# Where V's high and low parts lie in SBUF: interleaved, eight bytes between columns, in tiles half of 256 bytes further on

## The chip, the cores and the metric

The kernel runs on one core of a Trainium2 chip. The metric is device time in microseconds, the median of several executions. One execution is profiled; its rows are what the sections below quote.

## The reference

Eight batches of 3136 tokens go through an attention without softmax and then through a routed feed-forward part. Cut to what matters here:

```python
scores = (1 / S) * z @ z.T              # z: 3136 x 64
attn = np.maximum(scores, 0.0) ** 2     # 3136 x 3136
x = u * (attn @ v)                      # v: 3136 x 256
# then, per batch: the 128 tokens with the largest x @ w_gate go through
# relu(xe @ w1) @ w2, are weighted by a sigmoid, and are added back
```

By far the most work is in `attn @ v`: for each batch a product of 3136 x 3136 with 3136 x 256.

## The kernel before

Numbers are float32. To keep their precision in TensorE's faster float32 form, each operand is split into a high part and a low part (`split`: a copy that rounds gives the high part, a subtraction gives what is left). A product is then made of high times high, high times low and low times high, three matmuls that add into one PSUM bank.

Per batch, the tokens are cut twice. The columns of the score matrix are cut into seven chunks, five of 512 tokens, one of 256 and one of 320; a chunk is the moving operand's width of a matmul. The rows are cut into 24 pairs of 128-token tiles and a last half tile. One chunk with one pair of tiles is a slot, so there are 25 slots in a chunk. In each slot `scores` (line 440) makes the scores of a later slot, with slices of `ZH` and `ZL` as weights and a chunk of `Z` as the moving operand. ScalarE takes the relu and the square out of PSUM and rounds it (`hi`, lines 450 and 451), VectorE or GpSimd subtracts (`lo`, line 518). Since the score matrix is symmetric, about half of the squares are not computed again but stored to DRAM, transposed, and fetched back (`qk`, cast at line 418).

`mix` (line 556) then does the slot's twelve matmuls of `attn @ v`. V is the weight operand, 128 tokens by 128 features at a time; the squares `hi` and `lo` are the moving operand. For each of the two tiles and each half of the features there are three matmuls: V's high part with `hi`, V's low part with `hi`, V's high part with `lo`. Each matmul has a weight load of its own.

`prep_v` (lines 293 to 310) fills V. A tile of the pool `vpool` holds two token tiles: first the high parts of all 512 columns (2 x 256 features), then the low parts of the same columns, 2048 bytes each. ScalarE writes the high part, GpSimd the low part (for the first few tiles VectorE does). `V[b, j][:, w, h]` is what `mix` loads: part `w` (0 high, 1 low), feature half `h`, 128 columns that lie next to each other, 512 bytes.

Tiles are laid out pool after pool in the order in which the code makes them. Six constants (`c_sb`, `k_sb`, `w_bc`, `w_run`, `c16`, `w_col`) stand first in the pool `const`, then the expert's weights `wh` and `wl`, then `ZH`, `ZL` and `Z`, then `vpool`, and behind it the pools with `hi` and `lo`. Laid out so, `wh`, `wl`, `ZH`, `ZL`, `Z`, all twelve V tiles, `hi` and `lo` start at a multiple of 256 bytes within a partition.

The order of the instructions on each engine is written out by the program: a table of slots, with loads and preparations placed so many slots ahead, and all DMAs of the attention on SyncE's queue.

Of the kernel before, what the change touches and what calls it, by code (L numbers as in the profile page):

```python
# [10 lines left out]
F32 = mybir.dt.float32  # L11
F32R = mybir.dt.float32r
BF16 = mybir.dt.bfloat16
I32 = mybir.dt.int32
# [4 lines left out]
P = 128  # L19
CH = 512  # L20
GT = 4
Q = 32
# [66 lines left out]
def attention_then_routed_ffn(ctx: ExitStack, tc: tile.TileContext, zt, ut, v, wg, w1, w2, cst, cst16, keys, outs, at, cap):  # L89
# [8 lines left out]
    NK = D // P  # L98
# [10 lines left out]

    const = ctx.enter_context(tc.tile_pool(name="const", bufs=1))  # L110
    vpool = ctx.enter_context(tc.tile_pool(name="vpool", bufs=NJ // 2))
    stage = ctx.enter_context(tc.tile_pool(name="stage", bufs=2))
    work = ctx.enter_context(tc.tile_pool(name="work", bufs=2))
    tail = ctx.enter_context(tc.tile_pool(name="tail", bufs=2))
# [8 lines left out]
    def split(src, hi, lo, hi_on=None, lo_on=None):  # L123

        (hi_on or nc.scalar.copy)(hi, src)  # L125
        (lo_on or nc.vector.tensor_tensor)(lo, src, hi.bitcast(F32), op=ALU.subtract)  # L126
# [3 lines left out]
    staged = {}  # L130

    small = {
        "c_sb": const.tile([P, cst.shape[1]], F32, name="c_sb"),
        "k_sb": const.tile([P, keys.shape[1]], I32, name="k_sb"),
        "w_bc": const.tile([P, D], F32, name="w_bc"),
        "w_run": const.tile([P, RUN], F32, name="w_run"),
        "c16": const.tile([P, cst16.shape[1]], BF16, name="c16"),
        "w_col": const.tile([P, NK], F32, name="w_col"),
    }

    def load_consts():
# [59 lines left out]
    for o in range(0, W, 2 * D):  # L201
        kk, f = divmod(o, F)
# [16 lines left out]
    V = {}  # L219
# [74 lines left out]
    def prep_v(b, g, on=None):  # L294

        st = staged["v", b, g // 2][:, g % 2 * 2 :]
        n = 2 if 2 * g < NJ else 1
        if n == 2:
            t = vpool.tile([P, 2, NK, 2 * P], F32R, name="V", tag="V")
        else:  # L300
            t = vpool.tile([P, 2, NK, P], F32R, name="Vr", tag="Vr", bufs=1)
        src = st[:, :n].rearrange("p a d -> p (a d)").rearrange("p (f h i) -> p h f i", h=NK, i=Q)
        parts_of = [t[:, w].rearrange("p h (f i) -> p h f i", i=Q) for w in range(2)]
        lo_on, took = on or nc.gpsimd, {"dve": 1.0} if on else {"act": 0.6, "pool": 1.3}
        if not on and b == 0 and n == 2 and busy["pool"] + 1.3 > busy["dve"] + 0.6:
            lo_on, took = nc.vector, {"act": 0.6, "dve": 0.6}
        split(src, *parts_of, on and on.tensor_copy, lo_on.tensor_tensor)
        for q in range(n):
            V[b, 2 * g + q] = t[:, :, :, q * P : (q + 1) * P]
        spend(**took)  # L310


# [56 lines left out]
    def spend(act=0.0, dve=0.0, pool=0.0):  # L369
        busy["act"] += act  # L370
        busy["dve"] += dve
        busy["pool"] += pool
# [929 lines left out]
    for b in range(B):  # L1302
# [18 lines left out]
        for g in range(NJ // 2 + 1):  # L1321
            k = k0 - 10 + 3 * g // 2 if b else max(1, g - 3)
            if b or g > 3:
                at_slot(k, lambda b=b, g=g: prep_v(b, g))
            if (b or g > 6) and g % 2 == 0:
                load = (k - (3 if b else 2), lambda b=b, g=g: stage_v(b, g // 2))
                if b or 2 * g < NJ:
                    loads.append(load)
                else:
                    at_slot(*load)  # L1330
# [78 lines left out]
    def start():  # L1409
# [14 lines left out]
        prep_z(0, 1, hi_on=nc.vector.tensor_copy)  # L1424
        more_scores(0)
        prep_v(0, 0, nc.vector)
        busy["pool"] = 99.0
        settle_scores()
        more_scores(1)
        prep_v(0, 1)  # L1430
        square_scores()
        prep_z(0, 2, 1)
# [153 lines left out]
```

## Time and profile before

| | |
|---|---|
| median of 3 runs | 2068.55 us (2066.93 to 2069.06) |
| profiled execution, its time | 2067.41 us |
| its span, first to last instruction | 2065.6 us |
| TensorE busy, matmuls | 2055.2 us, 99% |
| TensorE busy, weight loads (beside the matmuls) | 1744.5 us, 84% |
| VectorE, ScalarE, GpSimd busy | 1529.0, 1291.2, 1357.5 us |

The busy time of matmuls is the time in which at least one is under way from its start to its modelled end, and a matmul starts while the one before it is still draining. So 99% says that there are almost no gaps; it does not say at what pace the matmuls follow each other. That pace is read from the starts of the rows of the timeline.

### The profile page before, as it was taken

The page shows a single profiled execution, that of the slowest core. Times are in us where ns is not written, and L with a number is a line of the kernel's source. Part 1 is how long each engine was busy: PE and PEld are TensorE (multiplying, and loading weights), DVE is VectorE, ACT ScalarE, POOL GpSimd, SP SyncE. Part 2 cuts the span into 40 slices and gives each one's busy share as a digit, 9 for nine tenths or more (in the row PEclk, how much of TensorE's full clock was granted, in tenths as well). Part 3 has the DMA queues.
Part 4 walks back from the last instruction along what each step waited for, and adds up shares of the span by engine and source line. Part 5 has one row for each costly group of instructions (what it writes and reads, how often), then busy time and mean ns, then how long its engine had stood idle before and what let it go on. Part 6 is the DMA issues. An engine that isn't in the chain of part 4 may idle for free.

```text
span 2065.6 us, 31660 instructions
## 1 busy us (share of the span) xinstructions
PE 2055.2 (99%) x10280; PEld 1744.5 (84%) x10280; DVE 1529.0 (74%) x2667; ACT 1291.2 (63%) x1629; POOL 1357.5 (66%) x728
## 2 busy tenths in 40 slices
PE   9999999999999999999999999999999999999999
PEld 6888988889888898888988889888898888888788
DVE  7676678856788667875678756887578876787776
ACT  7665576656775467664676546765477654775543
POOL 6766587756876468764677647875578755765643
PEclk9999999999999999999999999999999999999999
DMA  6788767886668765787767877678776776666862
GB/s 197 207 232 226 217 188 207 233 231 190 193 188 232 212 205 177 199 233 210 208 185 193 235 203 217 184 192 236 194 222 188 192 201 178 206 192 164 213 173 95
DMA packets 442758, 415.52 MB, mean 201 GB/s; under 512 B 133792, under 2 KB 374880, under 8 KB 439520
## 3 DMA queue, kind: packets, MB, share of 16 engines
q1 hardware_dynamic: 441456, 411.01, 70.9%
q0 software_dynamic: 768, 2.10, 0.3%
q8 instruction: 80, 1.31, 0.3%
q14 instruction: 86, 0.70, 0.1%
q10 hardware_dynamic: 368, 0.39, 0.1%
HBM read 238.78 MB, written 174.60 MB: 200 GB/s over the span
## 4 chain that ended last, share of the span: by engine, by line
PE 87%; DVE 3%; issue 2%; ACT 2%; DMA 2%; POOL 1%; SPq 1%; POOLq 0%; DVEq 0%; ACTq 0%
PE acc L556 73%; PE sc L440 12%; ACT hi L451 1%; POOL lo L518 1%; ACT a L450 1%; DVE a L462 1%; DVE aT L483 1%; PE h L1215 1%; PE y L1259 1%; DMA vst<-in_v 0%; DMA squares<-aT 0%; DVE lo L518 0%; DMA qk<-in_zt 0%; PE spread L680 0%; DMA qk<-squares_narrow 0%
## 5 line engine op out<-in xcount | busy, mean ns | idle before, releaser
L556 PE MATMUL acc<-hi,V 128*128 128x512 f32 (+2 forms) x5376 | 1218.4, 364 | 0.5
L518 POOL TENSOR_TENSOR lo<-a,hi 128x1024 fp32r<-128x1024 f32 (+2 forms) x326 | 717.9, 2204 | 563.5 <-DVE a L462 426.7
L556 PEld LDWEIGHTS acc<-hi,V 128*128 128x128 f32 x5376 | 932.9, 188 | 157.4 <-DVE ut L601 5.5
L556 PE MATMUL acc<-lo,V 128*128 128x512 f32 (+2 forms) x2688 | 664.0, 363 | 1.0 <-POOL lo L518 1.0
L450 ACT ACTIVATE a<-sc 128x1024 f32<-128x1024 f32 (+4 forms) x401 | 358.2, 893 | 449.2 <-PE sc L440 421.0
L556 PEld LDWEIGHTS acc<-lo,V 128*128 128x128 f32 x2688 | 471.1, 188 | 76.7 <-POOL lo L518 4.4
L462 DVE TENSOR_TENSOR a<-sc,a 128x1024 f32<-128x1024 f32 (+5 forms) x306 | 307.4, 1005 | 249.8 <-ACT hi L451 225.8
L418 ACT CAST hi<-qk 128x1024 fp32r<-128x1024 f32 (+2 forms) x327 | 279.7, 860 | 220.1 <-PE acc L556 198.1
L483 DVE STREAM_TRANSPOSE aT<-a 128x512 f32<-128x512 f32 (+3 forms) x541 | 349.5, 681 | 76.7 <-ACT a L456 54.4
L451 ACT ACTIVATE hi<-a 128x1024 fp32r<-128x1024 f32 (+4 forms) x401 | 372.2, 928 | 24.8 <-PE acc L556 2.3
L518 DVE TENSOR_TENSOR lo<-qk,hi 128x1024 fp32r<-128x1024 f32 (+2 forms) x220 | 319.2, 1459 | 81.7 <-ACT hi L418 79.3
L440 PE MATMUL sc<-Z,ZH 128*128 128x512 f32 (+2 forms) x746 | 275.1, 373 | 2.3 <-DVE a L462 2.1
L440 PE MATMUL sc<-Z,ZL 128*128 128x512 f32 (+2 forms) x746 | 273.3, 370 | 0.1
L518 POOL TENSOR_TENSOR lo<-qk,hi 128x1024 fp32r<-128x1024 f32 (+2 forms) x107 | 210.0, 1965 | 51.3 <-ACT hi L418 41.6
L440 PEld LDWEIGHTS sc<-Z,ZH 128*128 128x128 f32 x746 | 140.5, 188 | 31.7 <-DVE a L462 6.0
L440 PEld LDWEIGHTS sc<-Z,ZL 128*128 128x128 f32 x746 | 140.5, 188 | 24.7 <-DVE ZL L126 0.5
L126 POOL TENSOR_TENSOR V<-vst,V 128x512 fp32r<-128x512 f32 x92 | 136.5, 1489 | 29.8 <-ACT V L125 26.4
L622 POOL TENSOR_TENSOR ut<-x,w_run 128x1024 f32<-128x1024 f32 (+2 forms) x52 | 126.0, 2422 | 24.4 <-DVE x L613 23.4
L456 ACT ACTIVATE a<-a 128x1024 f32<-128x1024 f32 x93 | 98.8, 1062 | 2.9
L126 POOL TENSOR_TENSOR ZL<-zst,ZH 128x512 fp32r<-128x512 f32 (+2 forms) x56 | 84.2, 1508 | 2.5 <-ACT ZH L125 2.2
L125 ACT CAST V<-vst 128x512 fp32r<-128x512 f32 x95 | 57.9, 609 | 35.5 <-DMA vst<-in_v 35.5
L601 DVE SCALAR_TENSOR_TENSOR ut<-acc,ut 128x512 f32<-128x512 f32 (+2 forms) x112 | 63.9, 611 | 19.5 <-PE acc L556 19.2
(187 smaller groups left out, 1083.1 us busy)
## 6 DMA issues: line engine op xcount, KB each, us to landing
squares<-aT SPq DMA_DIRECT2D x160, 512.0 KB
qk<-squares SPq DMA_DIRECT2D x320, 256.0 KB
squares_narrow<-aT SPq DMA_DIRECT2D x320, 128.0 KB
qk<-squares_narrow SPq DMA_DIRECT2D x80, 512.0 KB
out<-x SPq DMA_DIRECT2D x162, 128.0 KB
ut<-in_ut SPq DMA_DIRECT2D x40, 512.0 KB
vst<-in_v SPq DMA_DIRECT2D x158, 128.0 KB
squares_own<-aT SPq DMA_DIRECT2D x39, 256.0 KB
```

Of the source, the lines that this page charges most:

```text
L126: (lo_on or nc.vector.tensor_tensor)(lo, src, hi.bitcast(F32), op=ALU.subtract)
L418: nc.scalar.copy(by(hi), src)
L440: nc.tensor.matmul(ps[:, q], z[:, j * P : (j + 1) * P], mov, start=z is ZH, stop=z is ZL)
L450: nc.scalar.activation(a, ps[:, :n], AF.Relu)
L451: nc.scalar.activation(pieces[0][0](hi), pieces[0][1], AF.Square)
L456: nc.scalar.activation(a, a, AF.Square)
L462: square = lambda: nc.vector.tensor_tensor(a[rows], of[rows, :n], a[rows], op=ALU.mult)
L483: nc.vector.transpose(to, a[rows, q].rearrange("p (m t a) -> p m t a", m=GT, a=Q))
L518: on.tensor_tensor(view(lo), src, view(hi).bitcast(F32), op=ALU.subtract)
L556: nc.tensor.matmul(ac[h], w, mov, start=first and h not in started, stop=stop)
L601: nc.vector.scalar_tensor_tensor(xT[:, h, :w], acc[b, c][h], SCALE * SCALE, xT[:, h, :w], op0=ALU.mult, op1=ALU.mult)
L622: nc.gpsimd.tensor_tensor(wx, runs, consts["wg_run"].rearrange("p (o r) -> p o r", o=1).broadcast_to([P, NB, RUN]), op=ALU.mult,)
```

## The change

The tile of V becomes `[P, NK, 2 * P, 2]`: the last axis is the part. The high part of a feature stands beside its low part, and the 128 columns that a weight load reads lie eight bytes apart, over 1024 bytes. ScalarE and GpSimd write the parts with the same step. The view that `mix` takes has its axes put back in the old order, so `mix` is unchanged.

Four of the six constants (`c_sb`, `k_sb`, `c16`, `w_col`; with padding 2208 + 160 + 800 + 32 = 3200 bytes, 12.5 times 256) go into a new pool `fixed`, made behind `vpool`. All that stood between, `wh`, `wl`, `ZH`, `ZL`, `Z` and the V tiles, moves 3200 bytes down and starts 128 bytes past a multiple of 256. The pools behind `fixed`, with `hi` and `lo`, stay where they were, at multiples of 256.

The instructions, their order on every engine, their sizes and what they wait for are the same as before.

```diff
     vpool = ctx.enter_context(tc.tile_pool(name="vpool", bufs=NJ // 2))
+    fixed = ctx.enter_context(tc.tile_pool(name="fixed", bufs=1))
...
-        "c_sb": const.tile([P, cst.shape[1]], F32, name="c_sb"),
-        "k_sb": const.tile([P, keys.shape[1]], I32, name="k_sb"),
+        "c_sb": fixed.tile([P, cst.shape[1]], F32, name="c_sb"),
+        "k_sb": fixed.tile([P, keys.shape[1]], I32, name="k_sb"),
...
-        "c16": const.tile([P, cst16.shape[1]], BF16, name="c16"),
-        "w_col": const.tile([P, NK], F32, name="w_col"),
+        "c16": fixed.tile([P, cst16.shape[1]], BF16, name="c16"),
+        "w_col": fixed.tile([P, NK], F32, name="w_col"),
...
         if n == 2:
-            t = vpool.tile([P, 2, NK, 2 * P], F32R, name="V", tag="V")
+            t = vpool.tile([P, NK, 2 * P, 2], F32R, name="V", tag="V")
         else:
-            t = vpool.tile([P, 2, NK, P], F32R, name="Vr", tag="Vr", bufs=1)
+            t = vpool.tile([P, NK, P, 2], F32R, name="Vr", tag="Vr", bufs=1)
...
-        parts_of = [t[:, w].rearrange("p h (f i) -> p h f i", i=Q) for w in range(2)]
+        parts_of = [t[..., w].rearrange("p h (f i) -> p h f i", i=Q) for w in range(2)]
...
         for q in range(n):
-            V[b, 2 * g + q] = t[:, :, :, q * P : (q + 1) * P]
+            V[b, 2 * g + q] = t[:, :, q * P : (q + 1) * P].rearrange("p h x w -> p w h x")
```

## Rows read from the trace of the kernel before

**Rows 1.** The page: busy time by engine; clock and DMA share in 40 slices.
```profile
PE 2055.2 (99%) x10280; PEld 1744.5 (84%) x10280; DVE 1529.0 (74%) x2667; ACT 1291.2 (63%) x1629; POOL 1357.5 (66%) x728
...
PEclk9999999999999999999999999999999999999999
DMA  6788767886668765787767877678776776666862
```

**Rows 2.** The page: the chain that ended last, by engine.
```profile
PE 87%; DVE 3%; issue 2%; ACT 2%; DMA 2%; POOL 1%; SPq 1%; POOLq 0%; DVEq 0%; ACTq 0%
```

**Rows 3.** Waits of PE: who waited for whom, us in total, times, longest.
```profile
PE sc L440 <- DVE a L462: 2.1, 4, 1.2
PE idle L1407 <- DVE zero L1404: 1.2, 1, 1.2
PE acc L556 <- POOL lo L518: 1.0, 2, 0.7
```

**Rows 4.** Timeline of PE, 512 wide: start us, us to the last end.
```profile
209.08 1.98 PE L556 MATMUL acc<-hi,V 128*128 128x512 f32 x8
210.89 1.07 PE L556 MATMUL acc<-lo,V 128*128 128x512 f32 x4
211.80 0.39 PE L556 MATMUL acc<-hi,V 128*128 128x512 f32 x1
```

**Rows 5.** Timeline of PE, 256 wide: first and last, 36 matmuls apart.
```profile
225.98 0.64 PE L556 MATMUL acc<-lo,V 128*128 128x256 f32 x4
...
230.30 0.28 PE L440 MATMUL sc<-Z,ZH 128*128 128x256 f32 x1
```

**Rows 6.** Timeline of PE, 320 wide.
```profile
1001.39 1.34 PE L556 MATMUL acc<-hi,V 128*128 128x320 f32 x8
1002.57 0.75 PE L556 MATMUL acc<-lo,V 128*128 128x320 f32 x4
1003.15 1.04 PE L556 MATMUL acc<-hi,V 128*128 128x320 f32 x6
```

**Rows 7.** Timeline of PE, 512 wide directly behind four of 256.
```profile
193.06 0.28 PE L440 MATMUL sc<-Z,ZL 128*128 128x256 f32 x1
193.19 1.09 PE L556 MATMUL acc<-lo,V 128*128 128x512 f32 x4
194.12 1.98 PE L556 MATMUL acc<-hi,V 128*128 128x512 f32 x8
195.93 1.07 PE L556 MATMUL acc<-lo,V 128*128 128x512 f32 x4
```

**Rows 8.** Timeline of PE: four transposes; the tile's rows: duration ns min/median/max.
```profile
437.09 0.60 PE L1231 MATMUL hT<-c_sb,hr 128*128 128x128 f32 x4
...
L1231 PE MATMUL hT<-c_sb,hr x64: 271/272/327, 437.1 to 2055.9; 128*128 128x128 f32 x64
```

**Rows 9.** Weight loads by shape: count, busy us, mean ns, idle before.
```profile
L556 PEld LDWEIGHTS acc<-hi,V 128*128 128x128 f32 x5376 | 932.9, 188 | 157.4 <-DVE ut L601 5.5 <-issue 1.3 <-ACT hi L418 0.8
L556 PEld LDWEIGHTS acc<-lo,V 128*128 128x128 f32 x2688 | 471.1, 188 | 76.7 <-POOL lo L518 4.4 <-issue 0.2
...
L556 PEld LDWEIGHTS acc<-hi,Vr 128*128 128x128 f32 x224 | 39.0, 189 | 6.1 <-issue 0.2
...
L1231 PEld LDWEIGHTS hT<-c_sb,hr 128*128 128x128 f32 x64 | 7.7, 140 | 1.8 <-ACT hr L1225 0.3
...
L719 PEld LDWEIGHTS gate<-c_sb,gate 128*98 128x98 f32 x14 | 2.3, 164 | 0.7
```

**Rows 10.** Timeline: two matmuls, and the weight loads that run beside them.
```profile
131.13 0.39 PE L440 MATMUL sc<-Z,ZH 128*128 128x512 f32 x1
131.36 0.39 PE L440 MATMUL sc<-Z,ZL 128*128 128x512 f32 x1
...
131.14 0.19 PEld L440 LDWEIGHTS sc<-Z,ZL 128*128 128x128 f32 x1
131.36 0.64 PEld L556 LDWEIGHTS acc<-lo,V 128*128 128x128 f32 x3
```

**Rows 11.** The tile V: who writes it, duration ns min/median/max.
```profile
L125 ACT CAST V<-vst x95: 597/605/623, 11.4 to 1806.4; 128x512 fp32r<-128x512 f32 x95
L126 POOL TENSOR_TENSOR V<-vst,V x92: 1267/1308/2322, 22.2 to 1810.5; 128x512 fp32r<-128x512 f32 x92
```

**Rows 12.** Busy time in two stretches: us, PE, PEld, DVE, ACT, POOL, clock, DMA share.
```profile
260.00:280.00 20.00, 19.94 (x87) 15.99 (x86) 17.16 (x23) 15.74 (x20) 19.61 (x12) 1.00 0.72 223
...
640.00:700.00 60.00, 60.00 (x273) 49.41 (x272) 40.77 (x54) 33.47 (x39) 31.01 (x15) 1.00 0.94 255
```

## Prediction

> **What bounds the kernel now.** I read the page first. Matmuls are under way 99% of the span at the full clock in every slice [rows 1], PE has 87% of the chain that ended last [rows 2], and PE's waits for other engines come to under 5 us [rows 3]. So the time is the number of matmuls times the pace at which they follow each other, and the reader is to look for that pace in the starts, not in the busy share.
>
> The timeline gives it. At 512 columns, 12 matmuls take 211.80 - 209.08 = 2.72 us, 226.7 ns each [rows 4]. At 256 columns, 36 take 230.30 - 225.98 = 4.32 us, 120.0 ns each [rows 5]. At 320, 12 take 1.76 us, 146.7 ns each [rows 6]. From 256 to 512 columns the price rises by 106.7 ns, 0.417 ns a column (one column per cycle at 2.4 GHz). What is left over is the same at each width: 226.7 - 213.3 = 13.3, 120.0 - 106.7 = 13.3, 146.7 - 133.3 = 13.3 ns. The change can only work on this leftover. Over the 8288 matmuls beside which a load of V or Vr runs (5376 + 2688 + 224 loads [rows 9]) it comes to 8288 x 13.3 = 110 us.
>
> What is the leftover? Two rows say that it is no fixed price of a matmul. First, it changes with what went before: right behind four matmuls of 256 columns, four of 512 take 194.12 - 193.19 = 0.93 us, 232.5 ns each, a leftover of 19.2; the next eight take 1.81 us, 226 each, so it is back at 13 [rows 7]. Something slides against something else and settles. Second, the transposes nearly lack it: four take 0.60 us, of which one's own 272 ns is the last, so (600 - 272) / 3 = 109 ns each for 128 columns [rows 8]. At two cycles a column that is 106.7 and a leftover of 2.6 (between 1 and 4 with the rounding of 0.60). They too load 128 new columns for each matmul, but their loads take 140 ns and not 188 [rows 9].
>
> What slides could be the two readers of SBUF. A load starts with the matmul before it (131.14 against 131.13, then both at 131.36) and runs beside it [rows 10]. A load of 128 columns takes 188 ns and one of 98 takes 164 [rows 9], so 24 / 30 = 0.8 ns a column, about two cycles. Before, the matmul therefore walks through its operand at 4 bytes a cycle and the load through V at 4 bytes in two cycles: the distance between the two keeps changing during a load, and whatever place makes them collide is passed again and again.
>
> **The change, part by part.**
>
> *Eight bytes between columns.* The load now walks 8 bytes in two cycles, 4 bytes a cycle, the pace of the matmul. The distance between them stays what it was at the start. If the leftover comes from collisions, it is now all or nothing, and a collision that delays one of the two shifts them apart for the rest of the load. What this saves isn't in the trace. From below: nothing. From above: all 13.3 ns, 110 us. I take the leftover of the transposes, the nearest row in which a load runs beside every matmul: 13.3 - 2.6 = 10.7 ns, times 8288 = 88.7 us. The other side, a loss, is not excluded either: the 128 columns now span 1024 bytes, twice as many, and if what is paid for is the span read, the leftover doubles, +13.3 ns x 8288 = +110 us.
>
> *128 bytes beside 256.* V moves against `hi` and `lo` by half of 256 bytes. In the trace all of these tiles start at the same place modulo 256, so no row prices it; with the fixed distance it decides which distance that is. It has the same bounds as the step, and I count no more for it. `Z`, `ZH` and `ZL` move together, so the 1492 score matmuls see the old distance and the old packed loads: 0.
>
> *Writing V.* ScalarE writes 95 high parts in 605 ns and GpSimd 92 low parts in 1308 [rows 11], now with a step. No row has such a write. From below 0; from above, each GpSimd instruction becomes as long as the longest in the row, 2322: 92 x 1.0 = 93 us of GpSimd time, of which 708 us is idle over the span (2065.6 - 1357.5 [rows 1]). It matters only where GpSimd is full, as at 260 to 280 us, 19.61 of 20 [rows 12]; if that cover is gone, PE waits for `lo`. I take 0, since both parts of a column still lie beside each other.
>
> *What takes over.* A PE that saves 88.7 of 2067 us wants everything 4.3% sooner. Where GpSimd has 19.61 us of work in 20, the stretch would shrink to 19.1; eight batches begin so, 8 x 0.5 = 4 us. In the stretch from 640 to 700 us, DMA is 0.94 busy [rows 12], and a like stretch of some 60 us comes once in each of seven batches: PE wants to save 60 x 4.3% = 2.6 us in each, 18 us in all, and transfers of `squares` and `qk` allow between all and none of it. I take half, 9 us. `lo` and `qk` are then late, and line 556 waits.
>
> Sum, against the profiled execution's own 2067.4 us: 2067.4 - 88.7 + 4 + 9 = 1991.7. The median of the runs is 1.1 us above that execution, so 1993.
>
> **What the skill says.** The Trainium skill, "TensorE: Matmul & The Clock Gate", Part 2 (step 1), says that PE has two independent read ports into SBUF and that loading the next weights takes no read bandwidth from the running matmul. By that rule the two streams can't collide, neither part of the change touches the pace, and the sum is 2068.6; rows 7 don't sit well with it, rows 4 to 6, one leftover at three widths, do. It is the second rival below. The Trainium skill, "SBUF — State Buffer", Door 1 (the box on cachelines), says that full bandwidth needs at least two accesses in each 16-byte line. Float32 columns 8 bytes apart have exactly two, so by this rule the load itself keeps its 188 ns and the sum stays; no row here has such a step.
>
> **The rivals.**
>
> *Slower: each load costs by its span.* Place: beside every V load, the running matmul is held up for a price per stretch of SBUF that the load touches, and the stretch is twice as long. For it: the leftover is equal at 256, 320 and 512 columns, so it goes with the load and not with the matmul, and loads of V all have one size. Against it: 19.2 and 13 with the same loads [rows 7]. If the leftover doubles: 8288 x 13.3 = +110, 2179 us; if half of that, +55, 2124. It decides as soon as the new leftover is above 13.3, each ns being 8.3 us.
>
> *No change: a fixed price.* The leftover is the handing over of weights, whatever the addresses. For it: the same 13.3 at three widths. Against it: rows 7 and the transposes. Time: 2068.6, within 4 us.
>
> *Half.* The new distance avoids some of the collisions, or the leftover settles at another value between 2.6 and 13.3, or GpSimd's stepped writes and the full DMA stretches take back more than I allow. At a leftover of 6.7: 8288 x 6.7 = 55 us saved, 2014; up to the edge of no change.
>
> **How the numbers follow.** Two compared kernels can be told apart here at about 0.2%, 4 us. My forecast (a leftover near that of the transposes, 1965 to 2003 us) has 0.38, the half case (2003 to 2064) 0.20, no change 0.14, slower by up to the half price (to 2125) 0.10, slower by more 0.18. So faster 0.58, same 0.14, slower 0.28. The predicted time is 1993. A range of 8 in 10 must leave out no more than 0.2: it drops the dear slower case (0.18) and a little below 1965 (0.02; the bound of 110 us saved lies at 1958), and reaches from 1965 to 2125. The forecast's own range is 1965 to 2003.
>
> **What the new profile would show.** If I am right: matmuls of 512 columns at line 556 start every 216 ns or so and those of 256 every 109, while those of line 440 that have a `ZL` load beside them keep 227; loads of V still take about 188 ns; PE's waits grow from 5 to some 15 us, for `lo` and for `qk`. If loads cost by span, the starts lie 240 ns apart. If the price is fixed, they stay at 227 and 120. V's writes at lines 125 and 126 should keep 605 and 1308 ns. Wrong I would be if the fixed distance happens to be a colliding one, so that the two stay stuck for the whole load; rows of before can't tell that, since none has two streams at one pace.

## The result, and the profile after

The change makes the kernel slower: 2094.43 us against 2067.84 us measured beside it, a ratio of 1.013 (95% interval 1.0113 to 1.0148). The forecast was 1993 us, so the direction was wrong. The time lies inside the range given, on its slower half.

The page of the kernel after (busy time by engine; granted clock in 40 slices; the chain that ended last):

```profile
PE 2084.5 (100%) x10280; PEld 1793.4 (86%) x10280; DVE 1527.1 (73%) x2667; ACT 1296.0 (62%) x1629; POOL 1359.4 (65%) x728
...
PEclk9999999999999999999999999999999999999999
...
PE 91%; ACT 3%; DVE 2%; issue 2%; DMA 1%; SPq 1%; POOL 1%; POOLq 0%; ACTq 0%; DVEq 0%
```

The span of this execution is 2094.5 us, 28.9 more than before. TensorE's busy time grew by 29.3 us against [rows 1], its share of the chain rose from 87 to 91% [rows 2]. The other engines did what they did before, and the clock is the same. So the matmuls themselves became longer. The page's costliest groups say which (busy us, mean ns, then idle time before):

```profile
L557 PE MATMUL acc<-hi,V 128*128 128x512 f32 (+2 forms) x5376 | 1236.0, 368 | 1.5 <-ACT hi L419 0.9
...
L557 PEld LDWEIGHTS acc<-hi,V 128*128 128x128 f32 x5376 | 966.0, 196 | 144.1 <-DVE ut L602 4.6
L557 PE MATMUL acc<-lo,V 128*128 128x512 f32 (+2 forms) x2688 | 672.0, 366 | 0.4 <-POOL lo L519 0.4
...
L441 PE MATMUL sc<-Z,ZH 128*128 128x512 f32 (+2 forms) x746 | 275.8, 374 | 1.8 <-DVE a L463 1.5
L441 PE MATMUL sc<-Z,ZL 128*128 128x512 f32 (+2 forms) x746 | 275.8, 374 | 0.0
```

Line numbers are one higher than before. The same four groups of matmuls on the page of before:

```profile
L556 PE MATMUL acc<-hi,V 128*128 128x512 f32 (+2 forms) x5376 | 1218.4, 364 | 0.5
...
L556 PE MATMUL acc<-lo,V 128*128 128x512 f32 (+2 forms) x2688 | 664.0, 363 | 1.0 <-POOL lo L518 1.0
...
L440 PE MATMUL sc<-Z,ZH 128*128 128x512 f32 (+2 forms) x746 | 275.1, 373 | 2.3 <-DVE a L462 2.1
L440 PE MATMUL sc<-Z,ZL 128*128 128x512 f32 (+2 forms) x746 | 273.3, 370 | 0.1
```

They grew by 17.6, 8.0, 0.7 and 2.5 us, together 28.8 beside the span's 28.9. The groups overlap where one follows the other, so this says where the time went and is not an exact account. A V load takes 196 ns in place of 188 [rows 9], still less than the 231 ns or so between two starts at 512 columns.

The mean of 368 ns is a duration that overlaps the next matmul's. The pace stands in the starts. PE's timeline of after (start us, us to the last end), first 512 columns wide, then 256:

```profile
126.18 1.09 PE L557 MATMUL acc<-lo,V 128*128 128x512 f32 x4
127.11 2.01 PE L557 MATMUL acc<-hi,V 128*128 128x512 f32 x8
128.96 0.39 PE L441 MATMUL sc<-Z,ZH 128*128 128x512 f32 x1
...
229.15 0.64 PE L557 MATMUL acc<-lo,V 128*128 128x256 f32 x4
...
233.50 0.28 PE L441 MATMUL sc<-Z,ZH 128*128 128x256 f32 x1
```

Twelve matmuls of 512 columns take 128.96 - 126.18 = 2.78 us, 231.7 ns each, where [rows 4] had 226.7. Thirty-six of 256 columns take 4.35 us, 120.8 ns each, where [rows 5] had 120.0. So the leftover over the columns rose from 13.3 to 18.3 ns at 512 and barely at 256. The single starts show more than the mean. Before, a settled train (matmuls directly one behind the other) steps by 226, 227, 227 ns and so on. After, it runs through a cycle of seven, 230, 228, 232, 232, 236, 229, 233 ns, again and again.

PE's waits (us in total, times, longest) and the two writers of V (min/median/max ns), both of after:

```profile
PE sc L441 <- DVE a L463: 1.5, 2, 1.2
PE acc L557 <- ACT hi L419: 0.9, 1, 0.9
PE acc L557 <- POOL lo L519: 0.4, 1, 0.4
```

```profile
L126 ACT CAST V<-vst x95: 641/657/682, 11.4 to 1832.9; 128x512 fp32r<-128x512 f32 x95
L127 POOL TENSOR_TENSOR V<-vst,V x92: 1287/1332/2332, 22.4 to 1836.8; 128x512 fp32r<-128x512 f32 x92
```

The waits did not grow from those of [rows 3]. The writes with a step cost 52 ns more on ScalarE and 24 on GpSimd than in [rows 11], 95 x 0.052 + 92 x 0.024 = 7 us on engines that have hundreds of microseconds to spare.

### The profile page after: what moved, and what is told of

Its sections match the earlier page's. It is cut to its first block, busy times and chain, and to the rows that moved or that the text cites. A ratio compares the mean times of both kernels' runs of the same rounds, so it can differ in the third digit from the quotient of the medians.

```text
span 2094.5 us, 31660 instructions
## 1 busy us (share of the span) xinstructions
PE 2084.5 (100%) x10280; PEld 1793.4 (86%) x10280; DVE 1527.1 (73%) x2667; ACT 1296.0 (62%) x1629; POOL 1359.4 (65%) x728
## 4 chain that ended last, share of the span: by engine, by line
PE 91%; ACT 3%; DVE 2%; issue 2%; DMA 1%; SPq 1%; POOL 1%; POOLq 0%; ACTq 0%; DVEq 0%
PE acc L557 75%; PE sc L441 13%; ACT a L451 1%; ACT hi L452 1%; DVE a L463 1%; PE h L1216 1%; PE y L1260 1%; DMA vst<-in_v 1%; POOL lo L519 1%; DMA qk<-in_zt 0%; DMA qk<-squares_narrow 0%; DVE aT L484 0%; PE spread L681 0%; ACT V L126 0%; SPq L289 0%
## 5 line engine op out<-in xcount | busy, mean ns | idle before, releaser
L557 PE MATMUL acc<-hi,V 128*128 128x512 f32 (+2 forms) x5376 | 1236.0, 368 | 1.5 <-ACT hi L419 0.9
L557 PEld LDWEIGHTS acc<-hi,V 128*128 128x128 f32 x5376 | 966.0, 196 | 144.1 <-DVE ut L602 4.6
L557 PE MATMUL acc<-lo,V 128*128 128x512 f32 (+2 forms) x2688 | 672.0, 366 | 0.4 <-POOL lo L519 0.4
L557 PEld LDWEIGHTS acc<-lo,V 128*128 128x128 f32 x2688 | 488.0, 196 | 70.0 <-POOL lo L519 1.1
L419 ACT CAST hi<-qk 128x1024 fp32r<-128x1024 f32 (+2 forms) x327 | 279.6, 859 | 229.7 <-PE acc L557 201.3
L126 ACT CAST V<-vst 128x512 fp32r<-128x512 f32 x95 | 62.7, 660 | 35.1 <-DMA vst<-in_v 34.9
L602 DVE SCALAR_TENSOR_TENSOR ut<-acc,ut 128x512 f32<-128x512 f32 (+2 forms) x112 | 63.9, 612 | 20.2 <-PE acc L557 19.9
```

What stands on the lines that cost most here:

```text
L419: nc.scalar.copy(by(hi), src)
L557: nc.tensor.matmul(ac[h], w, mov, start=first and h not in started, stop=stop)
L602: nc.vector.scalar_tensor_tensor(xT[:, h, :w], acc[b, c][h], SCALE * SCALE, xT[:, h, :w], op0=ALU.mult, op1=ALU.mult)
```

## The experiments

Three theories stood at the start. **Place:** how the weights lie and step against the moving operand decides how often the two collide, and this change hit a bad place. **Span:** a load costs by the stretch of SBUF that it covers. **Fixed:** the leftover is a price of each matmul, and something else was lost. The runs end at a fourth, in which the moving operand comes first. Below, **packed** weights lie in columns next to each other, **stepped** weights eight bytes apart, and a place is the start of a tile modulo 256 bytes. The recorded expectations call the theories by letters, and the letters shift: A is Span in e1, e2 and e4, and any reading beside the running matmul in e3 and e5. B is Place. C gives the step and the place a part each. D is Fixed. E to G come with the loops of matmuls.

### One half of the change at a time

`e1_step_only` keeps the eight-byte step and puts the four constants back in front (`c_sb` as shown, and `k_sb`, `c16` and `w_col` likewise), so everything starts at 0 modulo 256 again:

```diff
-        "c_sb": fixed.tile([P, cst.shape[1]], F32, name="c_sb"),
+        "c_sb": const.tile([P, cst.shape[1]], F32, name="c_sb"),
...
```

> The changed kernel with its six constants back in front, so that all tiles start at multiples of 256 bytes again and only the eight-byte step between V's columns is left. Theory A (a load pays by the span of SBUF that it walks through): the whole loss is here, about 2094 us, matmuls of 512 columns some 232 ns apart, loads of V 196 ns. Theory B (with the load at the matmul's own pace, the fixed distance decides, and 128 was a bad one): another pace than in the changed kernel, up to 216 ns apart and 1993 us if this distance is free of collisions. Theory C (the step and the place each do a part of it): between 2068 and 2094 us.

`e2_move_only` is the kernel before with the four constants behind V: packed columns, 128 bytes beside 256.

> The kernel before with only the four constants moved behind V: V packed as before, but at 128 past a multiple of 256. Theories A and B: no change, 2068 us and 226.7 ns apart, since a packed load walks past every distance anyway and reads no more. Theory C: a loss of its own, and the settled rhythm of 226.7 ns is gone.

Measured against 2067.6 us: e1 2100.89 us (ratio 1.0157, 1.014 to 1.0174), e2 2096.07 us (1.0137, 1.012 to 1.0154). Each half alone loses at least as much as both together (e2 by no more than the noise, e1 clearly more). So e1 lies above the 2094 us that theories A and C allowed it, and the loss of e2 was foreseen by theory C alone. The page's groups of e1:

```profile
L556 PE MATMUL acc<-hi,V 128*128 128x512 f32 (+2 forms) x5376 | 1241.3, 368 | 0.9 <-ACT hi L418 0.5
L556 PEld LDWEIGHTS acc<-hi,V 128*128 128x128 f32 x5376 | 956.5, 194 | 157.5 <-DVE ut L601 4.3
```

And of e2:

```profile
L557 PE MATMUL acc<-hi,V 128*128 128x512 f32 (+2 forms) x5376 | 1237.8, 368 | 0.7 <-DVE ut L602 0.3
L557 PEld LDWEIGHTS acc<-hi,V 128*128 128x128 f32 x5376 | 933.0, 188 | 174.7 <-DVE ut L602 5.0
```

In e2 the loads are as before, 188 ns over 512 bytes, and the matmuls are 19.4 us slower in this group alone. The span theory can't give that, so it is out as the account of this loss. Neither can a fixed price: the same instructions at another place run at another pace.

### The weights' step, and other places

`e3_step0` is the kernel before, but `mix` reads one column of V 128 times. `e4_step_at64` moves only `k_sb` and `w_col` behind V, so that the stepped V lies at 64 modulo 256. `e9_v_at192` does the same to the packed V of before with `c16` and `w_col`, so that it lies at 192. The edit of e3, its two main lines:

```diff
+    one = lambda x: x[:, :1].broadcast_to([P, P])
...
-                        todo.append((h, V[b, j][:, w, h], hi[:, q], False))
+                        todo.append((h, one(V[b, j][:, w, h]), hi[:, q], False))
```

> The kernel before, where each V load reads one column 128 times over (step 0) in place of 128 columns; the output is then not the reference's, all other work is the same. Theories A and B (the leftover of 13.3 ns is the load's reading beside the running matmul): it falls to 2 to 4 ns, matmuls of 512 columns start about 216 ns apart and the time is near 1985 us. Rival D (the leftover is the handing over of weights, the addresses only disturb its rhythm): 13 ns stay, 2060 to 2070 us.

> The changed kernel, but with only k_sb and w_col (192 bytes) behind V, so that V, Z, ZH and ZL start 64 bytes past a multiple of 256. Theory A: 2094 us, the place does not matter. Theory B: a pace of its own, which differs from that at 128 and at 0 by several ns. Theory C: between 2068 and 2094 us.

> The kernel before with only c16 and w_col (832 bytes) behind V: V packed, at 192 past a multiple of 256, hi and lo at 0. The loop of matmuls alone gave 228.9 ns there, against 226.7 at 0 and 232.4 to 233.5 at 128. If its paces carry over: about 2.2 ns more on the 5792 matmuls of 512 columns beside a load of V, 2068 + 13 = 2077 to 2086 us, and 229 ns at line 556. If the rhythm in the kernel is its own: like the move to 128, 2090 to 2098 us.

Measured: e3 2082.78 us (1.0075, 1.0058 to 1.0091), e4 2091.77 (1.0118, 1.0101 to 1.0135), e9 2083.12 (1.0074, 1.0057 to 1.0091). All lose. e9 lies where the loop of matmuls (below) had put it, e4 between the bounds of theory C, e3 above both values of its expectation (1985 us, and 2060 to 2070). So e3 speaks against my reading of collisions: a load that walks nowhere leaves 17.6 ns at 512 columns (mean of the starts), not less. At 256 columns it does leave less, 113.6 - 106.7 = 6.9 ns, so the load's addresses do matter to the pace, but not as a walk that has to be kept apart.

### Which distance counts

`e6_z_only` makes `fixed` between `Z` and `vpool`: V, `hi` and `lo` stay at 0, while `Z`, `ZH`, `ZL`, `wh` and `wl` go to 128. `e8_all_moved` makes it behind all other pools, so that everything, `hi` and `lo` too, goes to 128. V is packed in both. The pool as e6 makes it (in e8 the line stands behind the other pools):

```diff
     const = ctx.enter_context(tc.tile_pool(name="const", bufs=1))
+    fixed = ctx.enter_context(tc.tile_pool(name="fixed", bufs=1))
     vpool = ctx.enter_context(tc.tile_pool(name="vpool", bufs=NJ // 2))
```

> The kernel before with the four constants between Z and V: V, hi and lo at multiples of 256 bytes as before, only Z, ZH, ZL, wh and wl 128 past one. If the pace hangs on where V lies against hi and lo: 226.7 ns at line 556 stay settled, 2068 to 2072 us. If any disturbed matmul pulls the whole train out of its rhythm: matmuls of V lose it too, 2085 to 2096 us.

> The kernel before with the four constants behind all other tiles, so that everything, hi and lo too, starts 128 bytes past a multiple of 256; V packed. If the distance between V and the moving operand decides and not the place (in the loop of matmuls alone 64 and 64, 128 and 128, 192 and 192 all gave 226.7 ns): 2066 to 2070 us and 226.7 ns at line 556, as before. If the place itself counts: 2085 to 2096 us.

Measured: e6 2072.18 us against 2067.69 (1.0021, 1.0011 to 1.0031), e8 2069.38 against 2067.71 (1.0009, 0.9999 to 1.0018). The page's groups of e8:

```profile
L557 PE MATMUL acc<-hi,V 128*128 128x512 f32 (+2 forms) x5376 | 1218.3, 364 | 1.2 <-ACT hi L419 0.5
...
L557 PE MATMUL acc<-lo,V 128*128 128x512 f32 (+2 forms) x2688 | 664.2, 363 | 1.3 <-POOL lo L519 1.2
...
L441 PE MATMUL sc<-Z,ZH 128*128 128x512 f32 (+2 forms) x746 | 275.0, 373 | 2.4 <-DVE a L463 2.2
```

These are the numbers of before to 0.2 us. So it isn't the place of V that costs (in e8 it lies at 128, as in e2), but its place against `hi` and `lo`. In e6 only the borders between `mix` and `scores` see a new distance, and the run takes 4.5 us longer. The starts show most of it there: at 512 columns, a `mix` matmul followed by a `scores` matmul takes 232.6 ns in place of 227.1, and the other way round 232.1 in place of 227.2, some 320 pairs each, 3.3 us.

### The pace by itself

`e5_pace` and `e7_pace2` compute nothing of the reference. They are TensorE alone: twelve matmuls a round in the order of `mix`, five rounds (60 matmuls) in a row, three such stretches for a case, each behind one marker matmul of another width, so that it begins at another moment. A case sets the form of the weights, their place, and the columns, step and place of the moving operand:

```diff
+CASES = [(packed, off, 512, 1, 0) for off in range(0, 256, 32)]
+CASES += [(stepped, off, 512, 1, 0) for off in range(0, 256, 32)]
+CASES += [(form, off, 512, 1, 0) for form in (step0, step4, same) for off in (0, 128)]
+CASES += [(form, 0, n, 1, 0) for form in (packed, stepped, step0) for n in (256, 320, 384, 504, 500)]
+CASES += [(form, 0, 512, 0, 0) for form in (packed, stepped, step0)]
```

> Only TensorE works: 44 cases of 3 x 60 matmuls one behind the other in the order of line 556, each stretch behind one narrow matmul (128, 100 or 76 columns) that shifts its start; it computes nothing of the reference. Cases: packed and stepped V at 0 to 224 past a multiple of 256 bytes; V read with step 0, with 16 bytes between columns, and always the same 128 columns; other widths, 504 and 500 among them; a moving operand with step 0 or at another place. Theory E (the leftover is set by a rhythm of about 6.67 ns against which starts fall, and places and steps only decide at which of its marks the train settles): means between 220 and 240 ns that scatter with the place, in packed and stepped cases alike, no case near 216; widths of 504 and 500 columns, which are no multiple of 16, never settle. Theory A (reading beside the running matmul): step 0 and the same columns fall to 216 ns, stepped cases lie 10 ns or more above packed ones at each place. With a moving operand of step 0 there is nothing to collide with: 216 ns by a theory of collisions, unchanged if it is the handing over of weights.

> Again only TensorE, 3 x 60 matmuls in each case, nothing of the reference. Cases: weight loads of 128, 96, 64 and 32 columns; a moving operand that repeats each of 256 columns twice, so that it walks half as many bytes in the same 512 columns; V at places that are no multiple of 32 bytes; the moving operand moved in place of V; widths from 480 to 508; both operands bfloat16. Theory F (the moving operand, at 4 bytes a cycle, has no reading to spare, and what a weight load reads beside it is time lost): the repeated columns fall to about 217 ns at every place, stepped V too, bfloat16 likewise; loads of fewer columns leave less, about 3 + (leftover - 3) x columns / 128. Theory G (the moving operand loses its time at its own start, whatever is loaded): repeated columns fall too, but loads of 32 columns leave the same 13 and 19 ns. Moving the operand or moving V by the same bytes gives like paces if the distance between the two counts, and both of them moved by 64 gives nothing new.

PE's timeline of e5 (start us; line 84 is a stretch, line 87 the marker behind it), for five cases:

```profile
34.01 13.86 PE L84 MATMUL acc<-m,w 128*128 128x512 f32 x60
47.71 0.20 PE L87 MATMUL gap<-m,w 128*128 128x76 f32 x1
...
202.63 14.22 PE L84 MATMUL acc<-m,w 128*128 128x512 f32 x60
216.69 0.20 PE L87 MATMUL gap<-m,w 128*128 128x76 f32 x1
...
357.02 14.35 PE L84 MATMUL acc<-m,w 128*128 128x512 f32 x60
371.20 0.21 PE L87 MATMUL gap<-m,w 128*128 128x100 f32 x1
...
1447.90 13.26 PE L84 MATMUL acc<-m,w 128*128 128x512 f32 x60
1461.00 0.20 PE L87 MATMUL gap<-m,w 128*128 128x76 f32 x1
...
1553.11 13.98 PE L84 MATMUL acc<-m,w 128*128 128x256 f32 x60
1566.91 0.23 PE L87 MATMUL gap<-m,w 128*128 128x100 f32 x1
```

From the start of a stretch to its marker, 60 matmuls take 13.70 us with packed weights at 0, 14.06 with packed weights at 128, 14.18 with stepped weights at 0, and 13.10 when the moving operand is one column read 512 times. The last pair is a moving operand of 256 columns that lie eight bytes apart: 13.80 us, as long as 512 packed columns. The same view of e7 (lines 95 and 98), for loads of 32 columns only, for a moving operand that reads each of 256 columns twice, and for weights and moving operand both moved by 64 bytes:

```profile
145.68 14.06 PE L95 MATMUL acc<-m,w 128*32 128x512 f32 x60
159.58 0.21 PE L98 MATMUL gap<-m,w 128*128 128x100 f32 x1
...
354.90 13.16 PE L95 MATMUL acc<-m,w 128*128 128x512 f32 x60
367.90 0.21 PE L98 MATMUL gap<-m,w 128*128 128x100 f32 x1
...
1052.95 13.84 PE L95 MATMUL acc<-m,w 128*128 128x512 f32 x60
1066.63 0.21 PE L98 MATMUL gap<-m,w 128*128 128x100 f32 x1
```

That is 13.90, 13.00 and 13.68 us. The steady pace (mean of the last 35 starts to starts of each stretch, 512 columns unless named, ns):

| weights | moving operand | pace |
|---|---|---|
| packed at 0; 0 and 64, 128 or 192 for both | packed | 226.7 |
| packed at 32, 64, 96, 128, 160, 224 | packed | 232.4 to 234.3 |
| packed at 192 | packed | 229.0 |
| packed at 4, 8, 16, 24, 176, 184, 200, 208 | packed | 230.0 to 233.4 |
| packed at 240 | packed | 226.7 to 228.3 |
| packed at 0 | packed, at 16 or 128 | 231.6, 232.4 |
| packed at 16 | packed, at 16 too | 230.0 to 233.3 |
| the same 128 columns each time, at 0; at 128 | packed | 226.7; 232.4 to 233.5 |
| one column read 128 times, at 0 and 128 | packed | 231.6 |
| stepped at eight places, 32 bytes apart | packed | 230.0 to 235.6 |
| 16 bytes between columns (load 309 ns) | packed | 236.1 |
| loads of 96, 64, 32 columns at 0 (161, 134, 109 ns) | packed | 230.0, 230.0, 231.6 |
| loads of 96, 64, 32 columns at 128 | packed | 231.6, 229.3, 230.8 |
| packed or stepped, several places | 256 columns, each twice | 215.8 |
| packed at 0 and 128, bfloat16 | bfloat16 | 215.8 |
| packed, stepped, one column | one column 512 times | 217.2 |
| packed at 0 or stepped at 0 | 256, 320, 384 columns | 120.0, 146.7, 173.3 |
| one column read 128 times, at 0 | 256, 320, 384 columns | 113.3 to 116.7, 146.7, 175.0 |

Two things decide the settled pace at 512 columns. The first is how many new bytes the moving operand reads for each column: with half as many the leftover is 215.8 - 213.3 = 2.5 ns, at every place and step of the weights tried. The second, as long as it reads four new bytes for each column, is how the weights lie and step against it: packed weights leave 13.3 ns at the same place if that is a multiple of 64 bytes, and more nearly everywhere else. Fewer columns in a load don't take the leftover away: at place 0 they make it larger, at place 128 smaller by 1 to 4 ns.

Of the theories written for the loops none held whole. The same 128 columns and the single column did not fall to 216 ns (A). A width of 504 columns did settle, at 226.7 ns (E). Repeated columns fell as F and G had it, but shorter loads neither left less in proportion (F) nor left 13 and 19 ns unchanged (G).

The loop foretells the kernel. Mean start to start of the 512-wide V matmuls in each kernel's trace (V without `Vr`, some 5700 pairs, those under 243 ns):

| V against hi and lo | kernel | in the kernel | in the loop |
|---|---|---|---|
| packed, 0 | before | 227.4 | 226.7 |
| packed, 128 | e2 | 232.5 | 232.4 to 233.5 |
| packed, 192 | e9 | 229.7 | 229.0 |
| stepped, 0 | e1 | 233.2 | 233.3 to 235.6 |
| stepped, 64 | e4 | 231.2 | 230.0 |
| stepped, 128 | after | 231.5 | 231.4 |
| one column, 0 | e3 | 230.9 | 231.7 |

Packed at the same place is best at 512 columns, but not at every width. At 256 columns the same means are 119.9 ns before, but 118.7 in e2 and 117.3 in e9, where packed V lies at 128 and at 192 (after: 120.8). The loops timed other widths at place 0 only.

### Half of the moving operand's bytes, in the kernel

`e10_half_bytes` is the kernel before in which `mix` reads the first half of the squares' columns, each twice, so the output is not the reference's. It asks where the leftover comes from and, besides, what a faster TensorE would have been worth here.

```diff
-            nc.tensor.matmul(ac[h], w, mov, start=first and h not in started, stop=stop)
+            x = mov.shape[1] // 2
+            nc.tensor.matmul(
+                ac[h].rearrange("p (x o) -> p x o", o=2), w,
+                mov[:, :x].rearrange("p (x o) -> p x o", o=1).broadcast_to([mov.shape[0], x, 2]),
+                start=first and h not in started, stop=stop,
+            )
```

> The kernel before, where the moving operand of line 556 repeats each of the first half of its columns twice: as many columns, half the bytes read; the output is then not the reference's. The loop of matmuls alone fell from 226.7 to 215.8 ns. If the leftover is the price of reading 4 bytes a cycle: 216 ns at line 556, and up to 8288 x 10.8 = 90 us less, 1978 us, if nothing else takes over; what the DMA queues and GpSimd take back shows as the difference, 1978 to 2000 us. If the leftover in the kernel has another cause: 2060 us or more.

Measured: 2028.73 us (0.9808, 0.9791 to 0.9825). PE's timeline of e10, with its waits and the page's busy times below:

```profile
128.04 1.02 PE L557 MATMUL acc<-lo,V 128*128 128x512 f32 x4
128.90 1.89 PE L557 MATMUL acc<-hi,V 128*128 128x512 f32 x8
130.63 1.03 PE L557 MATMUL acc<-lo,V 128*128 128x512 f32 x4
```

```profile
PE ahead L900 <- DVE upto L893: 13.8, 6, 2.3
PE acc L557 <- POOL lo L518: 7.3, 8, 1.1
PE sc L440 <- DVE a L462: 3.5, 5, 1.3
PE acc L557 <- DVE ut L606: 3.5, 8, 0.7
```

```profile
PE 1986.7 (98%) x10280; PEld 1733.9 (86%) x10280; DVE 1534.3 (76%) x2667; ACT 1285.8 (63%) x1629; POOL 1339.4 (66%) x728
```

Twelve matmuls take 2.59 us, 215.8 ns each: the pace that I forecast for the change, reached by another road. The time missed its expectation of 1978 to 2000 us. TensorE's busy time falls by 2055.2 - 1986.7 = 68.5 us, but its idle time rises from 10.4 to 2026.7 - 1986.7 = 40.0 us, so the span gains 38.9 only.

The score matmuls did not share in it. Their operands and places are those of before, yet at 512 columns their mean start to start rose from 227.5 to 232.1 ns, some 5 us over about 1180 pairs. In e2, where `Z`, `ZH` and `ZL` moved together, one score matmul behind another likewise took 231.8 ns in place of 227.6. So in short runs of matmuls the place is not all: what ran before them counts too, as [rows 7] had shown.

## Why the prediction was wrong

**What bounds the kernel: right.** TensorE's pace did set the time. The four groups of matmuls grew by 28.8 us where the span grew by 28.9, the waits did not grow, and the paces of the loop, where nothing else runs, come back in the kernel to about a nanosecond.

**Eight bytes between columns: the step that failed.** I took the leftover of 13.3 ns for collisions of two readers that slide past each other, and expected that a load at the matmul's own pace would keep them apart and leave the 2.6 ns of the transposes, -88.7 us. The step alone (e1) costs 33 us: its leftover is 233.2 - 213.3 = 19.9 ns, not 2.6. The leftover hangs first on the moving operand: with four new bytes a column it is 13 to 23 ns at 512 columns, with half of that 2.5 (e5, e7, e10). A load of 32 columns, or of one column read 128 times, doesn't take it away. So the transposes of [rows 8] were the wrong nearest row. If they take a column in two cycles, as their 109 ns for 128 columns suggests, they read half as many bytes in a cycle, and by these runs that alone could leave 2.6 ns; it is not shown, since transposes themselves weren't tried. That this and the shorter load were both different in that row was in view, and I followed the one that suited the theory.

**128 bytes beside 256: failed too.** "I count no more for it" made the move a detail of the step. By itself (e2) it costs 28 us. The kernel before had the arrangement that settles at 226.7 ns for 512 columns, V packed and at the place of `hi` and `lo`, and no arrangement timed with the full moving operand was faster there; the change left it in both ways at once. The sentence that foretold this is the one on what would make the prediction wrong, a fixed distance that is a colliding one, with the size much smaller than all or nothing. That it came near was luck, not its mechanism: in e2 the load is packed, its distance to the matmul keeps changing in the sense of the prediction, and it loses as much. The size: the mean leftover of the 512-wide V matmuls went from 14.0 to 18.2 ns, 5700 x 4.2 = 24 us, and that of the 512-wide score matmuls from 14.1 to 17.8, 1190 x 3.7 = 4 us.

**Z, ZH and ZL together: 0, a small miss.** Moved without V (e6), they cost 4.5 us, 3.3 of them at the borders, where a Z load runs beside a `mix` matmul and a V load beside a `scores` matmul. After the change the score matmuls lost the 4 us above. In the prediction I had looked at them only with their own loads, and not at what runs before them.

**Writing V: 0, right.** The writes did not keep their 605 and 1308 ns, as I had it, but took 657 and 1332; that stayed hidden.

**What takes over: mis-sized, though not called on.** I gave back 13 us of 88.7. In e10, where the pace did fall to 215.8 ns, idle time took back 29.6 of 68.5 us. `lo` was late as I said (7.3 us), but the dearest wait is line 900, six times behind VectorE's routing work, which I had not priced. So by e10 the forecast pace would have given about 2029 us, not 1993, as an estimate: e10 also lost some 5 us at the score matmuls.

**The rivals.** The slower side came, in the part (up to the half price) to which I had given 0.10, and by another mechanism than the one written there. Only that part puts the time inside the range. Cost by span falls with e2 (packed loads, same loss) and with e3 (no span, no gain); that the leftover is equal at 256, 320 and 512 columns, which spoke for it, holds for weights at the place of before; with one column read 128 times it is 18.3, 13.3 and 7 to 10 ns at 512, 320 and 256 columns (e5). The fixed price falls with e2 against e8. Loads with a longer step do take longer (188, 196 and 309 ns for 4, 8 and 16 bytes), but the pace does not follow the load: trains with loads of 188 ns run at 226.7 or at 233 by place, and loads of 309 ns overlap one another in a train of 236.1. Whether those longest loads set that one pace isn't shown.

The Trainium skill, "TensorE: Matmul & The Clock Gate", Part 2 (step 1), has two independent read ports and a load that takes no read bandwidth from the running matmul. The runs show no read bandwidth lost in proportion to the load: with 32 columns in place of 128 the train takes 231.6 ns for 226.7 at place 0, and 230.8 for 232.4 to 233.5 at place 128 (e7). But that the running matmul is left alone, as I had drawn from it for the second rival, they don't bear out: the place of the weights alone moves the pace from 226.7 to 233 ns (e5, e2). The same page, "Wait — 56ns, not 53.3ns?", gives columns / 2.4 GHz + about 2.5 ns for a warm matmul. That is 215.8 ns for 512 columns, exactly what bfloat16 and the half-read moving operand show here; a float32 moving operand with each of 512 columns read once never came below 226.7.

**What stays open.** Why the same place modulo 256 is the good one isn't shown; it was only found to be so, with packed weights, at 0, 64, 128 and 192 of both, and not at 16 of both. Some of the settled paces are whole multiples of 6.67 ns: 226.7 = 34 of them, 120.0 = 18, 146.7 = 22, 173.3 = 26, and 233.3 = 35. That is one unit for each 16 columns (64 bytes of a partition) and two more, or three where it goes badly; 504 columns take the same 226.7 as 512. A read in pieces of 64 bytes, with two or three pieces lost at each change of operand, would look like this, but other widths (480 columns 216.7, 488 columns 225.7, 496 columns 223.4 ns) don't fall on such multiples, nor do places such as 192 (229.0), and no run tells it from other causes. How what ran before sets the pace of a short run of matmuls is open too. No arrangement tried with the full moving operand was faster than before at 512 columns, which are most of the kernel, and no kernel run with it was faster.

## What to carry to other kernels

Where TensorE's pace is the bound, with a float32 moving operand of 512 columns in the form used here, keep the weight tiles packed and at the same place modulo 256 bytes as the moving tiles, a multiple of 64, and look at the places again whenever a small constant goes into or out of a pool ahead of them: 3200 bytes of constants cost 28 us here without one instruction changed. Other widths can have another good place (256 columns: 117.3 ns in e9, 119.9 before). Read the pace from starts, not from busy shares or durations, and try a layout in a loop of matmuls alone first, since its paces came back in the kernel to about a nanosecond. When a row is used as the nearest price, list everything that differs between it and the case; each difference is a theory of its own.

## What the runs showed that was not expected

- A float32 moving operand with eight bytes between columns costs twice as much: 256 columns take 230 ns, as 512 packed ones do, and not 120 (e5). The Trainium skill, "SBUF — State Buffer", Door 1 (the box on cachelines), lets float32 columns two to a 16-byte line run at full bandwidth. The weight load nearly agrees (196 against 188 ns), the moving operand does not.
- Weights read with 16 bytes between columns load in 309 ns, those with 4 in 188 (e5).
- A moving operand that repeats each column runs at 215.8 ns at every place of the weights tried, packed or stepped (e7): the sensitivity to place showed only where a float32 moving operand reads new bytes for each column.
- Fewer columns in a weight load can make the train slower: 128, 96, 64 and 32 columns at place 0 give 226.7, 230.0, 230.0 and 231.6 ns. At place 128 they make it faster: 232.4 to 233.5, 231.6, 229.3 and 230.8 ns (e7).
